# A fused linear-attention and feed-forward kernel: one mask tile, u by a row, refitted fillers, one decay row by DMA, and a new order

## The chip, the cores and the metric

The kernel runs on one core of a Trainium2 chip. The core has five engines that work side by side, each through its own list of instructions in order: PE (TensorE, matrix products and transposes into PSUM), DVE (VectorE, elementwise work and reductions), ACT (ScalarE, exponentials, logarithms and copies), POOL (GpSimd, some elementwise work, and the issue of the loads that convert types) and SP (SyncE, which here issues transfers). Sixteen DMA engines move data for all of them. The metric is device time in microseconds (us). The kernel before takes 171.32 us, the median of three runs (171.07 to 171.39).

## What is computed

There are 4 batches, 8 heads, 768 tokens and 48 dimensions per head. For each batch and head a state of 48x48 is carried along the tokens:

```python
cur = einsum('bhd,bhe->bhde', u * k_t, v_t)
y_t = einsum('bhd,bhde->bhe', r_t, state + cur)
state = w_t[..., None] * state + einsum('bhd,bhe->bhde', k_t, v_t)
```

The result, as 3072 rows of 384, goes through `a = x @ w1`, `b = x @ w2`, `h = (a * b) @ w3`, `out = h @ w_out`, with an inner width of 1024. All tensors come and go in float32.

## The kernel before

**Units.** The 768 tokens are cut into six chunks of 128. A unit is one chunk of one or two batches. There are 13 (`UNITS`): units 0 and 1 are the first chunk of batch 0 and of batch 1 alone; every other unit holds two batches. Tiles have the chunk's 128 tokens on the partitions.

**Attention of a unit t.** Names are those of the steps in the code. `ln_t` (L402) takes the logarithm of the decays w. `cs_t` (L414) sums it along the tokens with a triangular matrix `LT`; in the same step, for units whose state is needed later, eight (or four) matmuls of one column (L419) sum over the whole chunk, and `pc_t` (L426) makes the chunk's decay factors from that, with the channels on the partitions. `ne_t` (L433) is exp of minus the sum and `KRk_t` (L438) multiplies k by it. For r there are two ways. Units in `RAW` form the sum transposed (`csT_t`, L451), its exponential (`et_t`, L457), transpose r itself (`trw_t`) and multiply (`KRw_t`). The others form `iw_t`, `rw_t`, `e_t` and `KRr_t` and then transpose (`trr_t` on PE with the copy `trre_t`, or `dtr_t`, a transposing DMA on SP, from unit 7 on). k goes the same way (`trk_t` and `trke_t`, or `dtk_t` from unit 8 on). `m_t_b` (L549) forms the 128x128 products of all eight heads of one batch, and a strictly triangular mask is laid on them: by one DVE product from PSUM (`msk_t_b`, L568), or by a copy on ACT (`mcp_t_b`) and a second step on POOL or DVE (`maff_t_b`). `rk_t`, `ruk_t`, `dg_t` and `dv_t` give the term with u. `ys_t` adds what the state gives, `yi_t_b` the products with v; `yb_t` puts y together (for the unit in `Y_PE`, PE adds the u term by `yd_t`, and `ybc_t` copies). y is transposed to `xT`, by `yt_t` and `xT_t` or by the transposing DMAs `dty_t_b`. `kv_t`, `T_t`, `S_t` and `Sb_t` carry the state.

**Feed-forward of a unit.** w3 and w_out are first multiplied into one matrix `w34`, block by block: four transposes of w3 in each `wt_f_h`, a copy `w3Te_f`, eight matmuls `wm_f` (L374) and a copy `w34e_f`. Then, per unit, `a_t_g` and `b_t_g` (L688) are products with w1 and w2, `asb_t_g` (ACT) copies a, `abT_t_g` (DVE, L698) multiplies both, `o_t_b` (L704) multiplies by `w34`, `osb_t_b` copies and `st_t_b` (SP) stores.

**The order.** The order of all steps on all engines is written out by hand in the string `ORDER` as `step@engine`; each engine executes its own steps in that order. `BANKS` gives every product its PSUM bank. `warmB@N` stands for N matmuls of zeros (128x512, L302) into bank B; nothing reads them. Loads are steps as well: `win_t`, `kin_t`, `rin_t`, `vin_t` (L329), `w1_h`, `w2_h`, `w3_h` and `wo`, nearly all on POOL's queue, which converts to bfloat16 on the way and issues them in order with POOL's other work. Unit 0's k, r and v are loaded in float32 on SP (`wide_k` and so on, L320) and converted by DVE (`kc_0`, `rc_0`, `vc_0`, L324). u is loaded into all 128 partitions (L294).

Of the kernel before, what the change touches and what calls it, by code (L numbers as in the profile page):

```python
# [37 lines left out]
BANKS = """
cs0=0 ct1=1 cs1=2 tr1=0 ct0=3 tr0=1 ct3=4,5 tk0=2 tk1=6 m0_0=0,1 cs3=2,3 M0_0=0 kv0=7 cs2=5,6 m1_0=0,1 M1_0=1 wt0=4
wt1=5 kv1=6 ct2=0,1 y1=2,3 tk3=0 yt1=2 y0=6,7 tr3=3 tr2=6 tk2=1 m3_1=3,4 m3_0=5,6 M3_0=0 m2_0=0,1 wt2=7 M2_0=1 y3=5,6  # L40
M3_1=2 wt3=0 m2_1=1,2 yt0=3 M2_1=3 wm0=4 wm1=1 wm2=7 wt4=4 wt5=2 y2=5,6 wm3=0 yt3=1 wm4=4 cs4=5,6 wm5=2 cs5=3,4 a0_1=1
yt2=0 kv2=7 a3_2=5 a1_1=6 sa0_1=0 kv3=0 sa1_1=1 tr4=1 a2_2=7 a2_3=6 tk4=0 tr5=3 sa2_3=2 b2_2=2 b2_3=1 b1_1=4 b3_2=6
b0_1=3 sa2_2=1 tk5=4 a1_0=7 a0_0=3 sa1_0=0 a3_0=2 sa0_0=1 a2_1=4 sa3_2=2 b0_0=7 sa2_1=2 m4_0=0,1 m4_1=5,6 M4_0=3
a3_3=3 M4_1=1 wt6=4 b1_0=7 sa3_0=1 y4=0,1 m5_0=5,6 M5_0=2 b2_1=2 sa3_3=0 wt7=7 a3_1=3 b3_0=5 cs6=0,1 b3_1=6 a2_0=7
wm7=2 sa3_1=2 ct6=4,5 sa2_0=1 yt4=3 cs7=0,1 kv4=6 kv5=7 a4_3=3 wm6=4 sa4_3=2 y5=0,1 m5_1=5,6 b4_0=7 M5_1=1 tr6=3
b4_3=2 tk6=5 b2_0=6 a4_0=4 cs8=2,3 sa4_0=2 b3_3=0 a4_2=1 a4_1=4 o0_0=5 sa4_2=2 sa4_1=0 m6_0=6,7 y6=2,3 m6_1=0,1 o2_0=4
M6_1=1 M6_0=2 cs9=0,1 yt5=6 o3_0=7 so0_0=0 so2_0=1 b5_1=6 b4_1=5 a5_1=4 a5_2=0 sa5_1=1 yt6=2 b4_2=1 tk7=3 kv6=4 kv7=5
o3_1=6 so3_0=2 a5_0=2 cs10=3,4 sa5_0=1 a6_3=7 sa5_2=0 b6_3=2 sa6_3=2 b5_0=1 a6_2=0 b5_2=5 a6_1=7 a5_3=1 sa6_1=2 b6_1=3
sa6_2=1 sa5_3=0 o1_0=4 so3_1=0 m7_0=0,1 so1_0=1 m7_1=5,6 y7=2,3 M7_0=1 kv8=7 M7_1=2 o4_0=4 b6_0=0 so4_0=3 cs11=5,6
b5_3=1 b6_2=4 a6_0=2 yt7=3 o5_0=1 a7_2=3 sa6_0=0 so5_0=0 a7_1=4 a7_0=7 sa7_2=1 b7_0=2 sa7_0=2 o2_1=1 a7_3=5 so2_1=1  # L50
sa7_1=2 m9_0=2,3 m8_0=6,7 sa7_3=0 m8_1=0,1 M9_0=2 o5_1=4 M8_1=1 M8_0=3 b7_2=5 so5_1=2 y8=2,3 y9=0,1 m9_1=6,7 M9_1=0
b7_3=4 o4_1=5 cs12=6,7 o6_0=4 so4_1=1 b7_1=2 o6_1=3 o7_1=2 so6_0=3 a8_3=0 so6_1=0 so7_1=2 a8_2=1 a8_0=5 sa8_3=2 b8_3=4
sa8_0=0 b8_2=3 sa8_2=1 b8_0=2 kv10=6 kv9=7 a8_1=0 a9_0=4 sa8_1=2 o7_0=5 b8_1=1 so7_0=1 sa9_0=1 a9_2=3 m10_0=6,7
sa9_2=0 m10_1=4,5 y10=0,1 M10_0=0 a9_1=2 b9_1=3 M10_1=2 sa9_1=2 b9_2=6 o8_1=7 m11_0=4,5 m11_1=2,3 y11=0,1 M11_0=2
o8_0=6 M11_1=0 b9_3=4 a9_3=5 sa9_3=0 a10_3=2 b10_3=3 sa10_3=2 a10_0=5 b10_2=0 sa10_0=0 b10_0=1 so8_1=0 b10_1=2 b9_0=4
so8_0=2 a10_1=3 a10_2=5 a11_3=4 sa10_2=1 a11_2=6 sa10_1=0 b11_2=1 sa11_2=2 o9_1=7 y12=5,6 so9_1=3 m12_1=0,1 m12_0=2,3
sa11_3=1 M12_1=0 o10_1=7 M12_0=2 a11_0=4 so10_1=2 a11_1=0 sa11_0=0 sa11_1=2 b11_1=1 b11_3=7 o9_0=2 b11_0=3 o10_0=4
so9_0=0 o11_1=3 so10_0=1 b12_3=4 so11_1=3 a12_2=2 a12_0=7 sa12_2=0 b12_2=1 sa12_0=1 a12_3=5 b12_0=6 sa12_3=2 a12_1=0
b12_1=3 sa12_1=0 o11_0=2 o12_1=3 so11_0=2 o12_0=4 so12_1=3 so12_0=2
"""  # L60
ORDER = """
table@ACT zeros@DVE u@SP win_0@POOL kin_0@SP rin_0@SP win_1@POOL vin_0@SP rin_1@POOL win_3@POOL kc_0@DVE padlw@DVE
padet@DVE ones@DVE kin_1@POOL mask1@DVE LT@POOL win_2@POOL ln_0@ACT rc_0@DVE rk_0@DVE warm0@18 cs_0@PE padr@DVE
kin_2@POOL padkr@DVE ln_1@ACT uc@ACT warm1@6 csT_1@PE w3_0@POOL pc_0@ACT cs_1@PE ruk_0@DVE et_1@ACT ne_0@ACT
vin_1@POOL pc_1@ACT I128@POOL mask@POOL warm3@9 trw_1@PE csT_0@PE trw_0@PE ln_3@ACT kin_3@POOL ne_1@ACT warm4@3
csT_3@PE KRk_1@DVE KRk_0@DVE rin_3@POOL rk_1@DVE warm6@2 trk_0@PE vc_0@DVE trk_1@PE KRw_1@DVE trke_0@ACT dg_0@DVE
rin_2@POOL et_0@ACT et_3@ACT KRw_0@DVE ruk_1@DVE w3_1@POOL warm7@8 m_0_0@PE trke_1@DVE ln_2@ACT cs_3@PE msk_0_0@DVE
wo@POOL kv_0@PE cs_2@PE vin_3@POOL m_1_0@PE pc_2@ACT ne_2@ACT msk_1_0@DVE warm4@2 wt_0_0@PE w3_2@POOL pc_3@ACT
wt_1_0@PE ne_3@ACT wt_0_1@PE dg_1@DVE vin_2@POOL kv_1@PE csT_2@PE S_0@DVE dv_0@DVE yi_1_0@PE et_2@ACT dv_1@DVE
win_4@POOL S_1@DVE warm7@3 yd_1@PE KRk_3@DVE ybc_1@ACT KRk_2@DVE warm7@2 trk_3@PE w3Te_0@ACT win_5@POOL Sb_0@DVE  # L70
yt_1@PE yi_0_0@PE wt_1_1@PE Sb_1@ACT yb_0@DVE trw_3@PE w3Te_1@ACT trke_3@DVE w1_1@POOL warm1@1 trw_2@PE KRw_3@DVE
trk_2@PE KRw_2@DVE warm4@1 m_3_1@PE rk_3@DVE warm7@1 m_3_0@PE trke_2@DVE mcp_3_0@ACT rin_4@POOL ruk_3@DVE warm7@4
m_2_0@PE wt_2_0@PE maff_3_0@DVE mcp_2_0@ACT ys_3@PE wt_2_1@PE msk_3_1@DVE xT_1@ACT maff_2_0@POOL warm0@1 wt_3_0@PE
warm1@1 wt_3_1@PE dg_3@DVE m_2_1@PE yt_0@PE mcp_2_1@ACT rk_2@DVE kin_4@POOL warm4@3 wm_0@PE ruk_2@DVE maff_2_1@POOL
yi_3_0@PE w3Te_2@DVE wm_1@PE w34e_0@DVE dv_3@POOL dg_2@DVE yi_3_1@PE w3Te_3@ACT wm_2@PE rin_5@POOL yb_3@DVE w34e_1@ACT
wt_4_0@PE xT_0@DVE wt_5_0@PE w2_1@POOL wt_4_1@PE w3Te_4@DVE warm0@1 yi_2_0@PE wm_3@PE kin_5@POOL w34e_2@DVE dv_2@DVE
wt_5_1@PE yi_2_1@PE ln_4@ACT w1_0@POOL w34e_3@DVE yt_3@PE wm_4@PE yb_2@DVE w3Te_5@ACT xT_3@DVE iw_4@ACT cs_4@PE
w2_0@POOL w34e_4@DVE wm_5@PE pc_4@ACT ln_5@ACT ne_4@ACT cs_5@PE w3_3@POOL a_0_1@PE e_4@ACT yt_2@PE pc_5@ACT iw_5@ACT
rw_4@DVE kv_2@PE vin_4@POOL a_3_2@PE ne_5@ACT xT_2@DVE KRr_4@DVE a_1_1@PE asb_0_1@ACT S_2@DVE win_6@POOL kv_3@PE
asb_1_1@ACT KRk_4@DVE trr_4@PE T_3@DVE e_5@ACT a_2_2@PE rw_5@DVE win_7@POOL trre_4@ACT a_2_3@PE KRr_5@DVE trk_4@PE  # L80
S_3@DVE w34e_5@ACT trr_5@PE asb_2_3@ACT rk_4@DVE vin_5@POOL b_2_2@PE Sb_3@ACT ruk_4@DVE trre_5@DVE b_2_3@PE b_1_1@PE
KRk_5@DVE rin_7@POOL b_3_2@PE abT_1_1@DVE b_0_1@PE dg_4@DVE asb_2_2@ACT trk_5@PE kin_6@POOL abT_0_1@DVE a_1_0@PE
trke_5@ACT abT_2_2@DVE a_0_0@PE abT_2_3@DVE asb_1_0@ACT a_3_0@PE rin_6@POOL asb_0_0@ACT trke_4@DVE a_2_1@PE
asb_3_2@ACT b_0_0@PE abT_3_2@DVE asb_2_1@ACT m_4_0@PE abT_0_0@DVE m_4_1@PE mcp_4_0@ACT a_3_3@PE msk_4_1@DVE wt_6_0@PE
Sb_2@ACT b_1_0@PE asb_3_0@ACT maff_4_0@DVE wt_6_1@PE ys_4@PE abT_1_0@DVE dv_4@POOL m_5_0@PE yi_4_0@PE msk_5_0@DVE
# [678 lines left out]
```

## Time and profile before

| | |
|---|---|
| median of three runs | 171.32 us |
| the profiled execution | 171.16 us |
| its span, first to last instruction | 169.4 us |
| PE, PE's weight loads, DVE, ACT, POOL: busy | 162.6, 122.0, 134.1, 89.5, 86.2 us |
| matmuls of zeros | 66, busy 19.9 us |
| moved by DMA | 25.63 MB, mean 151 GB/s |

A profile page has these parts: busy time of each engine; the span in 40 slices of 4.2 us with the busy share of each engine in tenths; the DMA queues; the chain of work that ended last, followed back from the end; the costliest groups of instructions, with mean duration and the idle time ahead of them. Matmuls are pipelined: the mean duration of a matmul in a group contains its latency, and the time that it costs PE is the distance from one start to the next (0.2155 us for 512 columns, 0.1625 for 384, 0.109 for 256, 0.056 for 128, and about 0.025 for very narrow ones, as rows of the chain have it: eight of 512 columns in 1.73 us, eight of 384 in 1.30, 24 of 256 in 2.62, eight of 128 in 0.45). Such a distance is called a slot below. The span leaves out 1.76 us of the profiled execution's time.

### The profile page before, as it was taken

Reading aid. Unit: us, or ns where it says so; the run is one execution under the profiler, and the core shown is the slowest. Engines: PE = TensorE matmul, PEld = TensorE weight load, DVE = VectorE, ACT = ScalarE, POOL = GpSimd, SP = SyncE. Lnnn points to the kernel's source line nnn. Section 1 sums busy time; section 2 is a strip of 40 time slices with the busy share of each in tenths; the row PEclk is TensorE's granted clock in tenths of the full one; section 3 lists DMA queues with packets and bytes.
Section 4 is the critical chain, followed back from the end, with each engine's and each line's share of the span. In section 5 each row is a group of like instructions: output and inputs, shape, how many; then the busy total and the mean of one; then the engine's idle time right before and its main releaser. Section 6 shows DMA issues by size and latency. Waiting matters only on the chain.

```text
span 169.4 us, 4733 instructions
## 1 busy us (share of the span) xinstructions
PE 162.6 (96%) x1998; PEld 122.0 (72%) x1998; DVE 134.1 (79%) x221; ACT 89.5 (53%) x151; POOL 86.2 (51%) x83
## 2 busy tenths in 40 slices
PE   7999999999999999999999999999999799999991
...
DMA  3999999999999999999959999959949944603313
GB/s 80 212 205 182 146 198 189 206 215 153 183 203 217 175 173 167 172 149 174 194 106 90 174 203 236 164 49 109 135 109 141 157 87 109 165 4 95 137 58 130
DMA packets 98837, 25.63 MB, mean 151 GB/s; under 512 B 90880, under 2 KB 96640, under 8 KB 98816
## 3 DMA queue, kind: packets, MB, share of 16 engines
...
## 4 chain that ended last, share of the span: by engine, by line
PE 73%; DVE 11%; DMA 7%; ACT 4%; issue 2%; POOL 1%; SPq 0%; DVEq 0%; ACTq 0%
PE banks L688 28%; PE banks L704 13%; PE banks L302 10%; PE banks L374 6%; DMA vin<-in_v_dram 5%; PE banks L549 3%; DVE abT L698 3%; PE banks L594 2%; PE banks L414 2%; PE banks L510 2%; PE banks L365 1%; DMA out_dram<-osb 1%; DVE dg L528 1%; ACT a_sb L693 1%; PE banks L647 1%
## 5 line engine op out<-in xcount | busy, mean ns | idle before, releaser
L688 PE MATMUL banks<-xT,w_bf 128*128 128x256 bf16 (+1 forms) x624 | 69.7, 264 | 0.5 <-DMA xT<-yb 0.4
L688 PEld LDWEIGHTS <-w_bf 128*128 128x128 bf16 x624 | 55.2, 98 | 7.8 <-issue 1.0
L693 ACT COPY a_sb<-banks 128x512 f32<-128x512 f32 x48 | 27.4, 594 | 27.8 <-PE banks L688 22.5
L698 DVE TENSOR_TENSOR abT<-a_sb,banks 128x512 bf16<-128x512 f32 x48 | 31.6, 681 | 10.4 <-PE banks L688 6.9
L704 PE MATMUL banks<-w,abT 128*128 128x384 bf16 x192 | 34.5, 326 | 0.1
L704 PEld LDWEIGHTS <-abT 128*128 128x128 bf16 x192 | 18.1, 98 | 10.7
L568 DVE TENSOR_TENSOR Mbf<-banks,mask 128x1024 bf16<-128x1024 f32 x17 | 20.4, 1219 | 1.6 <-PE banks L549 1.3
L302 PE MATMUL banks<-zeros 128*128 128x512 bf16 x66 | 19.9, 431 | 1.4 <-DVE zeros L243 1.3
L537 POOL TENSOR_TENSOR dv<-vin,dg 128x768 bf16<-128x768 bf16 x9 | 13.3, 1482 | 15.5 <-DMA vin<-in_v_dram 8.7
L709 ACT COPY osb<-banks 128x384 f32<-128x384 f32 x13 | 6.3, 482 | 21.7 <-PE banks L704 9.2
L329 POOL DMA_DIRECT2D win<-in_w_dram x13 | 15.0, 1157 | 1.1 <-POOLq L748 0.8
L329 POOL DMA_DIRECT2D rin<-in_r_dram x12 | 13.8, 1152 | 2.8 <-DMA w_bf<-in_moe_w_dram 2.5
L402 ACT ACTIVATE lw<-win 128x768 bf16<-128x768 f32 (+1 forms) x13 | 10.5, 811 | 8.7 <-DMA win<-in_w_dram 8.7
L329 POOL DMA_DIRECT2D vin<-in_v_dram x12 | 13.9, 1160 | 2.3 <-DMA w_bf<-in_moe_w_dram 0.9
L329 POOL DMA_DIRECT2D kin<-in_k_dram x12 | 13.8, 1153 | 1.7 <-issue 0.7
L612 DVE TENSOR_TENSOR yb<-banks,dv 128x768 bf16<-128x768 f32 (+1 forms) x12 | 11.1, 921 | 4.4 <-issue 1.8
L302 PEld LDWEIGHTS <-zeros 128*128 128x128 bf16 x66 | 6.5, 108 | 8.2 <-issue 3.8
L433 ACT ACTIVATE NEt<-banks 128x768 bf16<-128x768 f32 (+1 forms) x13 | 9.9, 765 | 3.6 <-PE banks L414 3.6
L663 POOL TENSOR_TENSOR Sst<-Tst,pc 128x384 f32<-128x384 f32 x4 | 3.7, 934 | 15.7 <-DVE Tst L655 15.6
L374 PE MATMUL banks<-wo_bf,w3T 128*128 128x384 bf16 x64 | 11.7, 325 | 0.0
L528 DVE TENSOR_REDUCE dg<-ruk 128x16 f32<-128x768 bf16 (+1 forms) x13 | 11.5, 881 | 0.0
L594 PEld LDWEIGHTS <-Mbf 128*128 128x128 bf16 x192 | 7.8, 96 | 2.5 <-issue 1.1
...
## 6 DMA issues: line engine op xcount, KB each, us to landing
out_dram<-osb SPq DMA_DIRECT2D x24, 192.0 KB, 2.1
...
kin<-in_k_dram POOLq DMA_DIRECT2D x11, 192.0 KB, 7.8
rin<-in_r_dram POOLq DMA_DIRECT2D x11, 192.0 KB, 8.4
vin<-in_v_dram POOLq DMA_DIRECT2D x11, 192.0 KB, 8.7
...
wo_bf<-in_moe_w_out_dram POOLq DMA_DIRECT2D x1, 768.0 KB, 13.5
```

The costliest lines, as they stand in the source:

```text
L302: nc.tensor.matmul(banks[:, at, :], lhsT=zeros[:, :C], rhs=zeros, start=True, stop=True)
L329: QUEUE[eng].dma_start(dst, src)
L374: nc.tensor.matmul(one(f"wm{fi}")[:, :DM], lhsT=w3T[fi % 2][:, gi, :], rhs=wo_bf[:, gi, :], start=(gi == 0), stop=(gi == FI - 1))
L528: nc.vector.reduce_sum(dgs, ruks, axis=AX.X)
L537: e.tensor_mul(dvs, vv, dgs[:, :, None].to_broadcast([C, bh, D]))
L568: nc.vector.tensor_mul(Mbf[bank[f"M{t}_{b}"]], mview(), mask.rearrange("s (j q) t -> s j q t", j=2))
L594: nc.tensor.matmul(o[:, h % 2, b, h // 2, :], lhsT=M[:, h % 2, h // 2, :], rhs=vv[:, b * H + h, :], start=(not c and b == 0 and h < 2), st ...
L612: nc.vector.tensor_add(ybs.rearrange("t b (q e d) -> t e (b q) d", e=2, d=D), yview().rearrange("t e (x d) -> t e x d", d=D), dvs.rearrang ...
L688: nc.tensor.matmul(o[:, f, :], lhsT=wt[:, di, fi * P:(fi + 1) * P], rhs=x[:, di, :T], start=(di == 0), stop=(di == DI - 1))
L693: copier(eng)(a_sb[bank[f"sa{t}_{g}"]], one(f"a{t}_{g}"))
L698: nc.vector.tensor_mul(ab[:, g * per:(g + 1) * per, :T], sa.rearrange("p (f t) -> p f t", t=T), one(f"b{t}_{g}").rearrange("p (f t) -> p f ...
L704: nc.tensor.matmul(one(f"o{t}_{b}")[:, :DM], lhsT=ab[:, fi, b * C:(b + 1) * C], rhs=w34[:, fi, :], start=(fi == 0), stop=(fi == FI - 1))
```

## The change

It has these parts:

- The mask is one 128x128 tile, made by DVE as `LT` minus the identity, and is read eight times in place of a tile of 128x1024 made by a memset and a POOL selection.
- u comes as one row of 384 values, is converted (`uc`), spread over the partitions by a matmul with a row of ones (`ub`) and copied (`ue`).
- Unit 0's float32 tiles and u lie in the space of two `abT` tiles that are used only later; `win_0` and `vin_0` and u are issued by SP, `win_1`, `rin_0` and `kin_0` by ACT, and the conversions of unit 0 are on ACT.
- Units 0 and 2 leave `RAW`; `Y_PE` is unit 0 in place of unit 1; six mask steps in place of seven go by way of a copy on ACT; there are four `a_sb` tiles in place of three.
- The one-column matmuls are a step of their own, `cc_t`. For unit 10 they are left out: `px_10` takes the exponential of the last 32 rows of the sum, and `pd_10` moves the last row to the partitions by DMA.
- The fillers are counted in units of 128 columns: `warmB@N` issues N/4 matmuls of 512 columns and one for the rest. Their number falls from 66 of 512 columns to 144 units of 128.
- `BANKS` and `ORDER` are new throughout. Some code is more general (`BLOCKS`, `DEPTH`) with the same result here.

```diff
-N_ASB = 3
+N_ASB = 4
-RAW = {0, 1, 2, 3, 6}
+RAW = {1, 3, 6}
+ROW_PC = {10}
-POOL_MASK = {(2, 0), (2, 1), (3, 0), (4, 0), (6, 1), (7, 1), (8, 1)}
-Y_PE = {1}
+POOL_MASK = {(3, 0), (5, 0), (6, 1), (7, 1), (9, 1), (11, 1)}
+Y_PE = {0}
...
-    mask = sb.tile([C, 2 * HP, C], BF, name="mask")
+    mask = sb.tile([C, C], BF, name="mask")
-    u_f = sb.tile([C, DM], F32, name="u_f")
-    wide = {(x, t): sb.tile([C, H, D], F32, name=f"wide_{x}{t}") for t in sorted(F32_IN) for x in "krv"}
+    late = [abT[2][i].rearrange("p f t -> p (f t)") for i in (N_AB[2] - 2, N_AB[2] - 1)]
+    u_r = late[0][0:1, 4 * DM:5 * DM]
+    late = [x.bitcast(F32) for x in late]
+    u_f = late[0][0:1, DM:2 * DM]
...
     @op("mask")
     def _(eng):
-        nc.gpsimd.affine_select(mask, mask, compare_op=Alu.is_gt, fill=0.0, base=0, channel_multiplier=-1,
-                                pattern=[[0, 2 * HP], [1, C]])
+        nc.vector.tensor_sub(mask, LT, I128)
...
-        nc.sync.dma_start(u_f, u.rearrange("h d -> (h d)").partition_broadcast(C))
+        QUEUE[eng].dma_start(u_f, u.rearrange("h d -> (h d)").rearrange("(p x) -> p x", p=1))
...
+    @op("ub")
+    def _(eng):
+        nc.tensor.matmul(one("ub")[:, :DM], lhsT=LT[0:1, :], rhs=u_r, start=True, stop=True)
+    @op("ue")
+    def _(eng):
+        copier(eng)(u_bc, one("ub")[:, :DM])
...
     def warm(at, n):
-        for _ in range(n):
-            nc.tensor.matmul(banks[:, at, :], lhsT=zeros[:, :C], rhs=zeros, start=True, stop=True)
+        while n > 0:
+            k = min(n, 4) * C
+            nc.tensor.matmul(banks[:, at, :k], lhsT=zeros[:, :C], rhs=zeros[:, :k], start=True, stop=True)
+            n -= 4
...
+            @op(f"px_{t}")
+            def _(eng):
+                dst = own(prow)[96:].rearrange("t (e d b q) -> t b q e d", e=2, b=nb, q=HP)
+                for b in range(nb):
+                    nc.scalar.activation(dst[:, b, :, :, :D], cs_view()[96:, b].rearrange("t (q e d) -> t q e d", e=2, d=D),
+                                         Act.Exp)
+            @op(f"pd_{t}")
+            def _(eng):
+                QUEUE[eng].dma_start(PC, own(prow)[C - 1:C])
...
-                    nc.vector.tensor_mul(Mbf[bank[f"M{t}_{b}"]], mview(), mask.rearrange("s (j q) t -> s j q t", j=2))
+                    nc.vector.tensor_mul(Mbf[bank[f"M{t}_{b}"]], mview(),
+                                         mask[:, None, None, :].to_broadcast([C, 2, HP, C]))
```

The opening of the old order, up to the first `wm`:

```
table@ACT zeros@DVE u@SP win_0@POOL kin_0@SP rin_0@SP win_1@POOL vin_0@SP rin_1@POOL win_3@POOL kc_0@DVE padlw@DVE
padet@DVE ones@DVE kin_1@POOL mask1@DVE LT@POOL win_2@POOL ln_0@ACT rc_0@DVE rk_0@DVE warm0@18 cs_0@PE padr@DVE
kin_2@POOL padkr@DVE ln_1@ACT uc@ACT warm1@6 csT_1@PE w3_0@POOL pc_0@ACT cs_1@PE ruk_0@DVE et_1@ACT ne_0@ACT
vin_1@POOL pc_1@ACT I128@POOL mask@POOL warm3@9 trw_1@PE csT_0@PE trw_0@PE ln_3@ACT kin_3@POOL ne_1@ACT warm4@3
...
rin_2@POOL et_0@ACT et_3@ACT KRw_0@DVE ruk_1@DVE w3_1@POOL warm7@8 m_0_0@PE trke_1@DVE ln_2@ACT cs_3@PE msk_0_0@DVE
wo@POOL kv_0@PE cs_2@PE vin_3@POOL m_1_0@PE pc_2@ACT ne_2@ACT msk_1_0@DVE warm4@2 wt_0_0@PE w3_2@POOL pc_3@ACT
...
warm1@1 wt_3_1@PE dg_3@DVE m_2_1@PE yt_0@PE mcp_2_1@ACT rk_2@DVE kin_4@POOL warm4@3 wm_0@PE ruk_2@DVE maff_2_1@POOL
```

The opening of the new order, up to the first `wm`, in full:

```
zeros@DVE win_1@ACT win_0@SP padlw@DVE ones@DVE rin_0@ACT u@SP LT@POOL kin_0@ACT vin_0@SP padr@POOL table@ACT
kin_1@POOL rin_1@POOL ln_1@ACT uc@DVE ln_0@ACT padkr@DVE warm0@33 cs_1@PE win_3@POOL ub@PE padpx@DVE cs_0@PE rc_0@ACT
csT_1@PE ue@DVE iw_0@ACT win_2@POOL cc_1@PE cc_0@PE ne_1@ACT ne_0@ACT e_0@ACT I128@POOL KRk_1@DVE kin_2@POOL kc_0@ACT
padet@DVE warm4@19 trk_1@PE et_1@ACT KRk_0@DVE trw_1@PE rw_0@DVE vc_0@ACT rin_3@POOL KRr_0@DVE pc_0@ACT trke_1@ACT
warm5@8 kv_0@PE rk_1@DVE trk_0@PE KRw_1@DVE rk_0@DVE warm6@3 m_1_0@PE vin_1@POOL ln_3@ACT ruk_0@DVE trr_0@PE S_0@DVE
trre_0@DVE trke_0@ACT rin_2@POOL warm7@6 cs_3@PE mask@DVE dg_0@DVE m_0_0@PE dv_0@DVE cc_3@PE ln_2@ACT kin_3@POOL
msk_1_0@DVE ne_3@ACT w3_0@POOL msk_0_0@DVE iw_2@ACT warm7@24 cs_2@PE w3_1@POOL ne_2@ACT ruk_1@DVE warm7@12 yi_0_0@PE
wo@POOL KRk_2@DVE yd_0@PE cc_2@PE ybc_0@ACT kv_1@PE vin_2@POOL e_2@ACT trk_2@PE yt_0@PE pc_3@ACT pc_2@ACT trke_2@ACT
csT_3@PE rw_2@DVE vin_3@POOL et_3@ACT win_4@POOL KRk_3@DVE Sb_0@ACT KRr_2@DVE warm1@27 trk_3@PE dg_1@DVE w3_2@POOL
trr_2@PE trke_3@ACT dv_1@DVE trw_3@PE win_5@POOL rk_3@DVE trre_2@ACT warm2@4 yi_1_0@PE wt_0_0@PE yb_1@DVE rin_4@POOL
wt_0_1@PE pc_1@ACT KRw_3@DVE wt_1_0@PE wt_1_1@PE S_1@DVE m_3_1@PE rk_2@DVE w3Te_1@ACT Sb_1@DVE msk_3_1@DVE w1_1@POOL
warm2@8 wt_3_0@PE w3Te_0@ACT wt_3_1@PE m_2_0@PE m_3_0@PE m_2_1@PE mcp_3_0@ACT msk_2_1@DVE xT_0@ACT yt_1@PE wt_2_0@PE
ruk_2@DVE ys_3@PE xT_1@DVE wt_2_1@PE dg_2@DVE kin_4@POOL wm_1@PE msk_2_0@DVE maff_3_0@POOL wm_0@PE w3Te_3@ACT dv_2@DVE
```

291 lines of the change are left out of this document (148 added, 143 removed).

## The prediction

> **What bounds the kernel now.** I read the page's busy times first, then the slices, then the chain that ended last, and then the timeline around the last of the filler matmuls.
>
> ```profile
> PE 162.6 (96%) x1998; PEld 122.0 (72%) x1998; DVE 134.1 (79%) x221; ACT 89.5 (53%) x151; POOL 86.2 (51%) x83
> PE   7999999999999999999999999999999799999991
> DMA  3999999999999999999959999959949944603313
> L302 PE MATMUL banks<-zeros 128*128 128x512 bf16 x66 | 19.9, 431 | 1.4 <-DVE zeros L243 1.3
> ```
>
> PE is never idle after the first slice, but 66 of its matmuls multiply zeros. They hold the places where it would wait. So PE's share does not say what bounds the first 31 us; the DMA row, full from the second slice on, suggests it. The chain in order of time (start us, us, what):
>
> ```profile
> 1.26 6.93 PE banks L302 x18
> ...
> 14.91 1.73 PE banks L302 x8
> ...
> 30.48 0.65 PE banks L302 x3
> 31.13 1.30 PE banks L374 x8
> ```
>
> The first 18 zeros take 0.385 us each, the eight at 14.91 us 0.216: PE starts at half pace (the granted clock reads 1.00 in every window all the same, so pace must be read from spacing). The last row is `wm_0`, the first matmul group that needs `wo`. After it only one zero matmul is left. The transfers around it, from the list of DMA issues (KB each, us to landing) and the timeline (start, us; the wait in brackets):
>
> ```profile
> u_f<-in_u_dram SPq DMA_DIRECT2D x1, 192.0 KB, 3.8
> wo_bf<-in_moe_w_out_dram POOLq DMA_DIRECT2D x1, 768.0 KB, 13.5
> 16.72 0.94 POOL L348 DMA_DIRECT2D wo_bf<-in_moe_w_out_dram  x1
> 30.48 1.16 POOL L329 DMA_DIRECT2D kin<-in_k_dram  x1 [0.53 <-DMA wo_bf<-in_moe_w_out_dram]
> ```
>
> `wo` is issued at 16.72 and lands 13.5 us later, at 30.2; POOL's next `kin` issue, which waits for that landing, confirms it. PE starts `wm_0` 0.9 us after. So the opening is bound by the queue of loads, and the zeros cover it. From there PE's own work runs nearly without a gap to 165.71 us, with DVE close behind (busy 49.2 of the 50 us from 60 to 110). PE's named waits:
>
> ```profile
> PE banks L594 <- DMA vin<-in_v_dram: 0.9, 1, 0.9
> PE banks L688 <- DMA xT<-yb: 0.4, 1, 0.4
> PE banks L688 <- DVE abT L698: 0.2, 1, 0.2
> ```
>
> Hence my sum: (start of the first `wm`) + (PE work after it) + (stalls after it) + (tail after the last matmul).
>
> **The change, part by part.** The sum is made against the profiled execution, 171.16 us (span 169.4 and 1.76 around it), 0.16 under the median.
>
> *Fillers.* Before: 66 × 0.2155 us = 14.2. After: fills of 144 units of 128 columns, or 36 matmuls' worth, 7.8 us. The 6.5 us less are not a gain by themselves: ahead of the first `wm` they only uncover waiting. Behind it, one zero matmul (0.22 us) goes: −0.22.
>
> *PE's real work.* Units 0 and 2 leave the raw path: 12 matmuls of `csT` go, 12 × 0.056 = 0.67 us. The eight one-column matmuls of `cc_10` go, 8 × 0.025 = 0.20. The row of `u` adds one of 384 columns, 0.16. Sum −0.71. In front of the first `wm` the order puts 10.20 us of real slots where it was 10.71, so behind it there is 0.20 less: −0.20.
>
> *Start of the first `wm`* (now `wm_1`). It needs `wo`. Ahead of `wo` the two kernels load the same tensors, in another order and partly by ACT and SP in place of POOL: all of units 0 and 1, `win`, `kin`, `rin` of 2 and 3, two quarters of w3. Only u changes, from 192 KB spread over 128 partitions to one row of 1.5 KB. Price of those 192 KB: above, the 1.05 us between u's landing and the next one on its queue (4.63 and 5.68); below, nothing, if they only filled the ramp of the first slice (3 tenths busy). I take 0.75, nearer the upper end, since 192 KB at the second slice's 212 GB/s is 0.9. So `wo` lands at 30.19 − 0.75 = 29.45, and `wm_1` starts 0.1 later, at 29.55 where it was 31.13: −1.58. That POOL issues its first load after two memsets (an estimate: 3.0 us where it was 1.35) costs nothing as long as the transfers of ACT and SP keep the engines full until POOL's land, 6.2 us after issue by the `win` of units 0 and 1; these six (u apart five of 192 KB at about 0.95 each, from the landings between 5.68 and 9.63) reach to about 8.5, POOL's first lands at about 9.2. If that gap is lost whole, 0.7 of the 1.58 is gone.
>
> *Is PE there by 29.55?* The last load its chain needs is `kin_3`. Before, everything up to `rin_2` had landed at 23.51; the same set without the first w3 quarter (2.12, from 15.77 to 17.89) and without u's 0.75 gives 20.6. Behind it DVE has, at the mean durations of their groups, KRk_3 0.61, KRr_2 0.70, dg_1 0.54, dv_1 0.55, rk_3 0.55, yb_1 0.56, KRw_3 0.69: 24.8. PE then has m_3_1, eight filler units and the steps up to `wt_2_1`: 0.29 + 0.43 + 2.24 = 2.96, so 27.8. It waits 1.7 us for `wo`. This is the cover for everything moved onto ACT and DVE in the opening (the three casts of unit 0 go to ACT at some 0.5 each; `ue`, rw and KRr of units 0 and 2 come to DVE, 0.55 + 0.71 + 1.35): they cost nothing until the chain slips by more than 1.7 us. On ACT, `ne_1` now queues behind `rc_0`, which waits for `rin_0`; everything on PE after `cc_0` waits for that. The slip is inside the 1.7 if `rin_0` lands by about 8.6, where it landed before.
>
> *DVE and ACT behind the opening.* By the rows DVE sheds the mask memset 0.91, casts 2.87, seven output copies 3.9, and gets one more PSUM mask (1.22); over all, DVE loses about 7.8 us of row time and ACT gains 9.5 on 89.5. The mask as one 128x128 tile read eight times costs nothing by the nearest row: ruk, which reads u over both batches, takes 557 ns against 549 for rk, which does not; above, if the repeat cost what it costs there per row, 18 × 0.01. Between 60 and 110 us, where DVE was full, its load falls only by about 1 in 54, so nothing is counted.
>
> *Row of unit 10.* ACT does two exponentials on 32 partitions (about 0.5 each) and SP one small transfer; the order places it 35 us of PE work ahead of `S_10`, so it is hidden.
>
> *Stalls behind the first `wm`.* Before: 165.71 − 31.13 = 134.58 of which slots take 132.1 (`a` and `b` 528 × 0.109 + 96 × 0.056 = 62.9, `o` 192 × 0.1625 = 31.2, `wm` 64 × 0.1625 = 10.4, all other steps in the order behind it 27.4, one zero 0.2), so 2.45. The 0.9 for `vin` goes: its issue stood 6.7 us of PE work ahead of its first use, now 18.5. What is late next are transfers with less slack, since PE arrives 1.6 us sooner at loads that land 0.75 sooner: `vin_3` (an estimate: 31.44, plus one more `vin` of 1.25 ahead of it, less 0.75: 31.9) feeds `yi_3_0` at 32.4; the third w3 quarter, now behind two `vin` and `win_4`, lands at 29.45 + 2 × 1.25 + 1.8 + 2.5 = 36.2, and PE wants it at 36.9. On SP, `dty_12_0` stands 3.3 us of PE work ahead of `a_12_0` and takes 2.6. Also POOL's mask step `maff_3_0` stands behind a `kin` issue that waits for `wo`, as before: ready at 32.2. All fit, by 0.2 to 0.7 us. I keep 2.45; ends: 1.2 (the two DMA waits go, none come) and 5 (as much again).
>
> *Tail* after the last matmul: unchanged, ACT copy and store.
>
> Sum: −1.58 − 0.20 − 0.22 + 0 = −2.0: 171.16 − 2.0 = **169.2 us**.
>
> **The rivals.**
> A. *Loads land no earlier* (the gap before POOL's first landing, or u's bytes were free). `wm_1` starts at 30.3; −0.83 − 0.42: 169.9. For it: the ramp slice is only 3 tenths busy.
> B. *PE falls back to half pace.* Before, PE was never idle for 1 us in the opening; now 6.5 us of filler are gone, with 1.7 us idle right before `wm_1`. If the pace drops, one slow stretch costs what the first one did: 6.93 − 18 × 0.2155 = 3.05 us, 172.2 us, slower. It decides once a stretch of about 2.1 us is lost at or after `wm_1`. For it: the new fills are sparse. Against: no row shows how long an idle stretch it takes. The Trainium skill, TensorE: Matmul & The Clock Gate, "Why this matters for your kernels", says that gaps up to about 3 us are safe, and its Part 4 that transposes do not count as activity; from 20.6 us to `wm_1` PE does mostly transposes, so by the first rule the sum stands, by the second B happens. No run shown can decide.
> C. *The new order stalls in the full stretch of DVE* (60 to 110 us): stalls at 5.0 in place of 2.45, 171.7. For it: DVE has nothing to spare there; against: its load is a little smaller.
> D. *Fewer stalls*: only 1.2, 167.9.
>
> **How the numbers follow.** Forecast (168.3 to 169.8) 0.42, A 0.13, D 0.10, C 0.20, B 0.15. About 0.2% (0.34 us) is what a measurement of this kernel can tell. Faster: forecast, A, D and a little of C, 0.67. Same: part of C, 0.07. Slower: B and the rest of C, 0.26. The range runs from D's lower edge, 167.6, to B with a small surplus, 172.4.
>
> **What would show it.** `wo` landing at 29.2 to 29.7 with `wm_1`'s first matmul right behind it and 1 to 2 us of PE idle ahead: the opening is right. `wo` at 30 or later: A. `w34` groups of eight taking 2.6 us in place of 1.30, or 0.107 us between 128-column matmuls after 20 us: B. PE waits for DVE's abT or a mask that sum to more than 3 us: C. The prediction is wrong from the root if PE reaches `wm_1` after `wo` has landed; then DVE's or ACT's chain bounds the opening, and each microsecond beyond 29.5 is one of the result.

## The result, and the profile after

The changed kernel takes **176.36 us** (median of 4 runs, 175.65 to 176.45); the kernel before took 171.28 beside it. The ratio is 1.029, with a 95% interval of 1.026 to 1.032: slower by 5.1 us, where 169.2 us was forecast. The profiled execution took 176.31 us, its span 174.6.

From the changed kernel's page: the busy times, and the slices of PE and of its clock.

```profile
PE 158.5 (91%) x1948; PEld 119.0 (68%) x1951; DVE 131.2 (75%) x210; ACT 97.2 (56%) x165; POOL 86.0 (49%) x83
PE   7699879999999999989993999799899989999991
PEclk9999999999999999999999699999999999999999
```

PE is busy for less time than before (158.5 against 162.6 us) in a longer span. Two things stand out: a slice at 3 tenths and the clock's 6 beside it, both between 91 and 100 us. The opening is not the place of the loss. Its timeline (start, us; the wait in brackets):

```profile
27.75 2.77 PE L400 MATMUL banks<-wo_bf,w3T 128*128 128x384 bf16 x16
28.00 1.19 POOL L355 DMA_DIRECT2D kin<-in_k_dram  x1 [2.92 <-DMA wo_bf<-in_moe_w_out_dram]
```

`wo` lands at 27.71 (issued 13.73, 13.98 later) and the first `wm` starts at 27.75; the timeline before has it at 30.97 (the chain, which leaves out what overlaps, at 31.13). To see where that gain went I compared the two traces at equal amounts of real matmul work left (start-to-start slots, zeros at nothing). After minus before, in us and good to some tenths, since the order of the work differs: −3.4 at the first `wm`, −2.9 at 50, −2.0 at 76, −0.6 at 90.5, +1.2 at 94.8, **+3.9 at 100.4**, **+5.2 at 110.8**, +6.3 at 128, +5.3 at the end. So the opening gained more than forecast; 2.8 of it went in small waits up to 90 us; and about 6 us were lost between 90 and 111.

That stretch, in the timeline of the changed kernel:

```profile
84.07 1.57 ACT L460 ACTIVATE prow<-banks 32x384 f32<-32x384 f32 x2
...
85.67 0.48 ACT L751 COPY osb<-banks 128x384 f32<-128x384 f32 x1
...
86.17 0.36 SPq L756 DMA_DIRECT2D out_dram<-osb  x1
86.36 1.22 POOL L355 DMA_DIRECT2D win<-in_w_dram  x1
...
86.65 3.29 SPq L532 DMA_TRANSPOSE KRT<-KR  x2
...
94.44 0.62 PE L592 MATMUL banks<-KRT 64*128 64x128 bf16 x16 [2.26 <-DMA KRT<-KR]
...
94.49 0.56 DVE L527 TENSOR_TENSOR KR<-rw,Et 128x768 bf16<-128x768 bf16 x1 [3.08 <-DMA KRT<-KR]
```

The first line is `px_10`, the two exponentials of the row of unit 10. Behind them on ACT stands `osb_1_0`; behind that, on SP, its store and the DMA transposes `dtr_7` and `dtr_8`. At 86.36, just ahead of `dtr_7`, POOL issues the load `win_12`. The chain in order of time has the price (start, us, what):

```profile
85.60 1.05 PE banks L746 x7
86.65 7.75 DMA KRT<-KR
...
94.49 0.42 DVE KR L527
```

`dtr_7` takes 7.75 us to land; before, its two transposes took 4.2 and 4.7. PE waits 2.26 us for it at `m_7`. Worse, DVE waits 3.08: `KRr_9` writes the `KR` buffer that `dtr_7` still reads (there are two). The order of work around this place, which the prediction had looked at only for `px_10`'s own cover:

```
asb_5_0@ACT Sb_5@ACT ys_6@PE dg_7@DVE osb_0_0@ACT dv_6@POOL o_1_0@PE ne_10@ACT px_10@ACT maff_6_1@DVE yi_6_0@PE
a_5_1@PE abT_5_3@DVE yi_6_1@PE osb_1_0@ACT o_3_0@PE ruk_8@DVE asb_5_1@ACT st_1_0@SP yb_6@DVE dtr_7@SP b_5_1@PE
Sb_6@DVE rw_9@DVE yt_6@PE dtr_8@SP osb_3_0@DVE b_4_2@PE dv_7@POOL xT_6@DVE o_2_0@PE abT_5_1@DVE st_3_0@SP st_3_1@SP
win_12@POOL dg_8@DVE st_0_0@SP b_5_0@PE pd_10@SP osb_2_0@ACT abT_4_2@DVE dtk_8@SP iw_10@ACT a_6_3@PE KRr_9@DVE
```

### The profile page after: what moved, and what is told of

It reads as the page before. It is cut to its first block, busy times and chain, and to the rows that moved or that the text cites. A ratio compares the mean times of both kernels' runs of the same rounds, so it can differ in the third digit from the quotient of the medians.

```text
span 174.6 us, 4648 instructions
## 1 busy us (share of the span) xinstructions
PE 158.5 (91%) x1948; PEld 119.0 (68%) x1951; DVE 131.2 (75%) x210; ACT 97.2 (56%) x165; POOL 86.0 (49%) x83
## 4 chain that ended last, share of the span: by engine, by line
PE 52%; DMA 17%; DVE 11%; POOL 8%; ACT 5%; issue 3%; SPq 1%; ACTq 0%; DVEq 0%
PE banks L730 26%; PE banks L746 13%; DMA vin<-in_v_dram 9%; DMA KRT<-KR 4%; DMA out_dram<-osb 4%; DVE abT L740 4%; PE banks L400 4%; PE banks L638 2%; POOL rin L355 2%; ACT a_sb L735 2%; POOL kin L355 1%; SPq L666 1%; POOL win L355 1%; DVE Mbf L611 1%; ACT NEt L476 1%
## 5 line engine op out<-in xcount | busy, mean ns | idle before, releaser
L730 PE MATMUL banks<-xT,w_bf 128*128 128x256 bf16 (+1 forms) x624 | 70.8, 265 | 3.0 <-DVE Mbf L611 1.2
L746 PE MATMUL banks<-w,abT 128*128 128x384 bf16 x192 | 35.7, 334 | 0.0
L746 PEld LDWEIGHTS <-abT 128*128 128x128 bf16 x192 | 18.6, 100 | 11.2 <-issue 1.0
L751 ACT COPY osb<-banks 128x384 f32<-128x384 f32 x20 | 9.5, 480 | 27.6 <-PE banks L746 19.3
L611 DVE TENSOR_TENSOR Mbf<-banks,mask 128x1024 bf16<-128x1024 f32 x18 | 21.7, 1218 | 2.8 <-PE banks L592 2.8
L580 POOL TENSOR_TENSOR dv<-vin,dg 128x768 bf16<-128x768 bf16 x10 | 15.8, 1585 | 12.0 <-DVE dg L571 7.7
L355 POOL DMA_DIRECT2D win<-in_w_dram x11 | 13.0, 1186 | 0.6 <-issue 0.5
L327 PE MATMUL banks<-zeros 128*128 128x512 bf16 (+3 forms) x35 | 10.5, 419 | 1.5 <-DVE zeros L258 1.3
L592 PE MATMUL banks<-KRT 64*128 64x128 bf16 x192 | 8.2, 218 | 2.5 <-DMA KRT<-KR 2.3
L606 POOL TENSOR_SCALAR_AFFINE_SELECT Mbf<-Mbf 128x1024 bf16<-128x1024 bf16 x4 | 4.5, 1131 | 10.9 <-ACT Mbf L598 10.9
L481 DVE TENSOR_TENSOR KR<-kin,NEt 128x768 bf16<-128x768 bf16 (+1 forms) x13 | 7.9, 604 | 2.4 <-DMA kin<-in_k_dram 2.1
```

Source lines behind the costliest of these rows:

```text
L327: nc.tensor.matmul(banks[:, at, :k], lhsT=zeros[:, :C], rhs=zeros[:, :k], start=True, stop=True)
L355: QUEUE[eng].dma_start(dst, src)
L580: e.tensor_mul(dvs, vv, dgs[:, :, None].to_broadcast([C, bh, D]))
L611: nc.vector.tensor_mul(Mbf[bank[f"M{t}_{b}"]], mview(), mask[:, None, None, :].to_broadcast([C, 2, HP, C]))
L730: nc.tensor.matmul(o[:, f, :], lhsT=wt[:, di, fi * P:(fi + 1) * P], rhs=x[:, di, :], start=(di == 0), stop=(di == DI - 1))
L746: nc.tensor.matmul(one(f"o{t}_{b}")[:, :DM], lhsT=ab[:, fi, k * C:(k + 1) * C], rhs=w34[:, fi, :], start=(fi == 0), stop=(fi == FI - 1))
```

## The experiments

Theory: the load and the transposes in flight together cost the time. Rivals: the fall of the clock; the row of unit 10 itself; the opening. Each ratio is to runs of the kernel before on the same chip; their medians are 171.1 to 171.4 us, so times from different chips can be compared to about 0.3 us. A time is the median of a run's executions; everything from a trace is of one of them.

**1. The load out of the way.**

```diff
-win_12@POOL dg_8@DVE st_0_0@SP
+dg_8@DVE st_0_0@SP
...
-vin_7@POOL abT_4_1@DVE
+vin_7@POOL win_12@POOL abT_4_1@DVE
```

> The changed kernel with one step moved: POOL issues win_12 right behind vin_7 (about 76.6 us) in place of behind dv_7 (86.36 us, 0.3 us ahead of SP's dtr_7). Theory T: PE's wait of 2.3 us for KRT, DVE's wait of 3.1 us for the KR buffer, and the lower granted clock behind them (0.64 and 0.51 in 96 to 100 us) all come from dtr_7 and dtr_8 landing 7.75 and 6.99 us after issue, because win_12's load moves at the same time. Then dtr_7 lands within 5 us of its issue, PE's wait for KRT is under 0.5 us, the granted clock stays at 1.00, and the time is 171.5 us (170.5 to 172.7). Rival R: the order on DVE is too slow there whatever the transposes do; the wait turns into one for DVE and the time stays above 174.5 us.

170.22 us (169.81 to 170.31), ratio 0.994 (0.991 to 0.996). Timeline:

```profile
86.57 2.71 SPq L532 DMA_TRANSPOSE KRT<-KR  x2
...
92.03 0.62 PE L592 MATMUL banks<-KRT 64*128 64x128 bf16 x16
```

The row of unit 10 is still there and SP issues the transposes at the same time, but they land in 3.1 to 3.3 us and nothing waits at `m_7`. The time is 0.3 us below the expected band. One moved load turns 5 us slower into 1 us faster.

**2. Zeros in the wait**, so that PE does not rest (44 units of 128 columns ahead of `m_7_0`).

```diff
-rk_9@DVE m_7_0@PE
+rk_9@DVE warm5@44 m_7_0@PE
```

> The changed kernel with 11 matmuls of zeros (512 columns, 2.4 us) put right ahead of m_7_0, where PE stands idle for 2.3 us. They can't shorten the wait. If the fall of the granted clock behind it follows from PE's idling, the clock stays at 1.00, the matmuls from 96 to 100 us run at full pace and the time falls by 1.2 to 2.0 us, to 174.3 to 175.1. If the clock has nothing to do with it, 176.3 within 0.4.

174.85 us (174.79 to 175.08), ratio 1.022 (1.019 to 1.024): inside the expected band, 1.5 us below the changed kernel, with the clock at 1.00 throughout. That seemed to price the clock's fall at 1.5 us; the traces say otherwise. At equal work left, this run is 1.5 us ahead of the changed kernel at first (98.94 against 100.44), but level with it three microseconds on (102.26 against 102.38) and up to 119 (118.83 against 118.92), because here PE then waits for DVE (PE's waits from 90 to 112 us: in us total, times, longest):

```profile
PE banks L730 <- DVE Tst L700: 1.2, 1, 1.2
PE banks L730 <- DVE Mbf L611: 1.2, 1, 1.2
```

In the changed kernel the first of these waits is missing: PE is late enough by itself. So the fall was hidden behind DVE. The 1.5 us at the end came later: the changed kernel's PE loses 0.75 us at 123.5, waiting for a transposing DMA of y, and 0.96 at 142.3, waiting for an output copy on ACT that itself waits 2.89 us for a store; this one does neither. Why not is left open.

**3. u's bytes back**: a second load of u, spread over 128 partitions as before, that nobody reads.

```diff
+    u_pad = sb.tile([C, DM], F32, name="u_pad")
+    @op("upad")
+    def _(eng):
+        QUEUE[eng].dma_start(u_pad, u.rearrange("h d -> (h d)").partition_broadcast(C))
```

> The changed kernel with one load more: u into all 128 partitions, 192 KB, on SP behind the row of u; nothing reads it. It prices the part of the change that narrows u. By the prediction's term wo lands 0.75 us later (27.7 becomes 28.4) and wm_1 starts as much later; the end is 0 to 0.75 us later, 176.3 to 177.1. By rival A the bytes are free, wo lands at 27.7 within 0.2 and the time is 176.3.

`wo` lands at 28.83 instead of 27.71, 1.12 us later. In the eleven traces that load as the changed kernel does, `wo` lands anywhere from 27.55 to 28.44 (mean 27.85), so the 192 KB are worth about 1 us, and no nearer than 0.4 to 1.3: not free, and my 0.75 is inside. The time, 175.87 us (175.74 to 177.26), is not above the changed kernel's, and below both expected bands: a microsecond gained in the opening is gone by the wait at `m_7`, where `dtr_7` lands at 95.06 here.

**4. The row of unit 10 undone**: the column form of the prefix for unit 10, as before; no `px_10`, no `pd_10`.

```diff
-ROW_PC = {10}
+ROW_PC = set()
...
-cs_10@PE abT_4_3@DVE
+cs_10@PE cc_10@PE abT_4_3@DVE
-ne_10@ACT px_10@ACT maff_6_1@DVE
+ne_10@ACT pc_10@ACT maff_6_1@DVE
-b_5_0@PE pd_10@SP osb_2_0@ACT
+b_5_0@PE osb_2_0@ACT
```

> The changed kernel with unit 10's decay factors made as before (cc_10 right behind cs_10, pc_10 in the place of px_10, no pd_10 and no padding of prow). pd_10 stands on SP between the transposes and the stores of the slow stretch. If it and the two exponentials on 32 partitions cost nothing, as predicted, 176.3 within 0.4 us; if they hold up SP or ACT there, 0.5 to 1.5 us faster.

169.73 us (169.22 to 171.32, 9 runs, four of them 170.7 or more), ratio 0.994 (0.990 to 0.997): far below either expectation. Timeline:

```profile
84.64 0.48 ACT L751 COPY osb<-banks 128x384 f32<-128x384 f32 x1 [0.45 <-PE banks L746]
...
85.14 0.36 SPq L756 DMA_DIRECT2D out_dram<-osb  x1
...
85.62 2.76 SPq L532 DMA_TRANSPOSE KRT<-KR  x2
...
86.22 1.22 POOL L355 DMA_DIRECT2D win<-in_w_dram  x1
```

Without the exponentials `osb_1_0` comes a microsecond sooner, and SP's transposes are issued 0.6 us ahead of the load instead of 0.3 behind it: `dtr_7` lands in 3.23 us. So the row that I had priced at nothing is worth 6.6 us here. Whether by its delay or by itself, the next three runs tell.

**5. Only the order**: the row stays, `px_10` goes behind `osb_1_0`.

```diff
-ne_10@ACT px_10@ACT maff_6_1@DVE
+ne_10@ACT maff_6_1@DVE
...
-osb_1_0@ACT o_3_0@PE
+osb_1_0@ACT px_10@ACT o_3_0@PE
```

> The changed kernel with one move: unit 10's two exponentials (px_10, 1.57 us on ACT) are issued behind osb_1_0 instead of ahead of it, so osb_1_0, its store on SP and the transposes dtr_7 and dtr_8 queued behind that store come about 1.5 us sooner, ahead of win_12's load. The row of unit 10 stays, with its DMA pd_10. Theory (order decides: what costs the time is that dtr_7 is issued behind the load): dtr_7 issued near 85.1, landing 3.1 to 3.5 us later, no wait at m_7, and the time 169.6 to 171.2 us. Rival (the row itself costs it: its exponentials and its DMA, wherever px_10 stands): 175 to 176.5 us.

169.74 us (169.41 to 170.43), ratio 0.991 (0.988 to 0.993).

```profile
84.58 0.48 ACT L751 COPY osb<-banks 128x384 f32<-128x384 f32 x1 [0.52 <-PE banks L746]
...
85.08 1.57 ACT L460 ACTIVATE prow<-banks 32x384 f32<-32x384 f32 x2
85.08 0.36 SPq L756 DMA_DIRECT2D out_dram<-osb  x1
...
85.56 2.74 SPq L532 DMA_TRANSPOSE KRT<-KR  x2
...
86.35 1.22 POOL L355 DMA_DIRECT2D win<-in_w_dram  x1
```

The same exponentials and the same DMA, one step further down ACT's queue, cost nothing that can be measured.

**6. Only the delay**: run 4 with two exponentials of the same shape in `px_10`'s old place, into a tile that nobody reads.

```diff
-ne_10@ACT pc_10@ACT
+ne_10@ACT pad_10@ACT pc_10@ACT
```

> The kernel with the row of unit 10 undone (169.73 us; no exponentials of a row, no pd_10), plus two exponentials of the same 32x384 shape in px_10's old place that write to a tile nobody reads: only the delay on ACT ahead of osb_1_0 is put back. Theory (the delay alone does it: it puts dtr_7 a fraction of a microsecond behind win_12's issue, and then transposes and load run together and land late): dtr_7 issued near 86.7, landing 6.5 us or more later, a wait of 1.5 us or more at m_7, and 174 to 176.8 us. Rival (the row's own DMA, or its tile, has to be there too): 169.5 to 171 us.

173.22 us (172.87 to 174.55), ratio 1.013 (1.008 to 1.018): 3.5 us over run 4, so the delay alone brings the wait back, but only half of the 6.6 us. In the profiled execution some 0.6 us of that has another source: `wo` lands at 28.34 in it, and the first `wm` starts 0.6 us later than in run 4's. Load and transposes are issued at the same moment here (86.92 and 86.91), and `dtr_7` takes 6.07 us:

```profile
86.91 3.15 SPq L541 DMA_TRANSPOSE KRT<-KR  x2
86.92 1.22 POOL L355 DMA_DIRECT2D win<-in_w_dram  x1
...
93.07 0.56 DVE L536 TENSOR_TENSOR KR<-rw,Et 128x768 bf16<-128x768 bf16 x1 [1.10 <-DMA KRT<-KR]
```

**7. Is the other half `pd_10`?** The changed kernel with `pd_10` issued behind `dtr_9`.

```diff
-b_5_0@PE pd_10@SP osb_2_0@ACT
+b_5_0@PE osb_2_0@ACT
...
-dtr_9@SP cs_11@PE
+dtr_9@SP pd_10@SP cs_11@PE
```

> The changed kernel with one move: pd_10, the DMA that spreads the row of unit 10 (issued at 92.05 on SP, landing 97.05), is issued behind dtr_9 instead, when the transposes of units 7 and 8 have landed. The delay alone gave 173.22 us, the changed kernel 176.36. Theory (the delay's exact place makes the difference: the load issued 0.29 us ahead of dtr_7 and not with it, transposes landing 7.75 us after their issue and not 6.07, then the clock's fall): the time stays at 175.5 to 176.6 us. Rival (pd_10's DMA in flight with them costs the rest): 173 to 174.5 us.

176.45 us (176.08 to 178.25), ratio 1.032 (1.026 to 1.039): no. With the load again 0.29 us ahead, `dtr_7` takes 7.86 us and DVE waits 3.2. What is left to tell 173.22 from 176.36 is the offset of load and transposes, 0.01 us against 0.29; no run puts the load 0.3 us ahead without the row, so that half is argued from the landing times and not isolated.

**8. The load further ahead**: run 4 with `win_12` ahead of `dv_7`.

```diff
-dv_6@POOL o_1_0@PE
+dv_6@POOL win_12@POOL o_1_0@PE
...
-win_12@POOL dg_8@DVE
+dg_8@DVE
```

> The kernel with the row of unit 10 undone (169.73 us), and one move the other way: win_12's load stands ahead of dv_7 on POOL, so it is issued near 84.6 instead of 86.22, about a microsecond ahead of dtr_7 (85.6). Theory (a load issued just ahead stretches the transposes): dtr_7 lands 6 to 8 us after its issue instead of 3.23, a wait of 1.5 us or more comes back at m_7, and the time is 173 to 176.5 us. Rival (the row of unit 10 was the cause and the load's place means nothing): 169.4 to 170.3 us, dtr_7 landing in under 4 us.

My expectation fell: 170.02 us (169.90 to 170.16), ratio 0.993. The load is issued at 84.44, 1.29 us ahead of `dtr_7`, which does take longer (5.44 us), but lands at 91.17. DVE comes to `KRr_9` only at 92.10 here, and at 91.19 in run 4, where PE comes to `m_7` at 91.97. So a stretched transpose costs nothing until it passes the moment at which DVE wants the buffer, 91.2 to 92.1. The load moves mostly before the transposes do: the list of DMA packets has 214 KB of it in flight from 87 to 88 us, ahead of nearly all of theirs.

Put together, for `dtr_7` and its load (offset is the load's issue minus `dtr_7`'s):

| kernel | offset, us | `dtr_7` to landing | lands at | DVE waits | time, us |
|---|---|---|---|---|---|
| load out of the way | far ahead, landed | 3.27 | 89.84 | 0 | 170.22 |
| px_10 behind osb_1_0 | +0.79 | 3.20 | 88.75 | 0 | 169.74 |
| row undone | +0.60 | 3.23 | 88.84 | 0 | 169.73 |
| delay only | +0.01 | 6.07 | 92.98 | 1.10 | 173.22 |
| changed | −0.29 | 7.75 | 94.40 | 3.08 | 176.36 |
| zeros in the wait | −0.30 | 7.75 | 94.31 | 3.1 | 174.85 |
| pd_10 late | −0.29 | 7.86 | 94.76 | 3.2 | 176.45 |
| u's bytes back | −0.30 | 8.03 | 95.06 | 3.4 | 175.87 |
| load further ahead | −1.29 | 5.44 | 91.17 | 0 | 170.02 |

In runs 10 to 12 below, `dtr_7` is again issued 0.6 us ahead of the load, and lands in 3.19 to 3.24 us.

**9. All loads earlier.** Run 4 with `win_12` as in run 1, and `vin_11` and `vin_12` moved up, away from the later transposes.

```diff
-vin_10@POOL m_9_1@PE
+vin_10@POOL vin_11@POOL m_9_1@PE
...
-rin_12@POOL S_8@DVE
+rin_12@POOL vin_12@POOL S_8@DVE
```

> The kernel with the row of unit 10 undone, win_12's load right behind vin_7's, and vin_11 and vin_12 right behind vin_10 and rin_12 (issued near 104 to 107 instead of 117.9 and 119.1), so that no load is in flight with the transposes of units 11 and 12 either. Theory (transposes in flight with loads are what still costs around 120 to 137): KRT landings there 3.1 to 4.2 instead of 4.1 to 6.2 us, and 168.9 to 169.6 us. Rival (nothing waits for them there; the waits left are those of DVE and ACT): 169.5 to 170.1 us.

A miss: 172.15 us (171.69 to 172.58), ratio 1.006 (1.003 to 1.008). At equal work left this trace is behind run 4's by 1.0 us at 106, 2.2 at 110, 2.9 at 122 and 3.1 at the end. So most was lost before any transpose was waited for, and to something else: each issue of a load keeps POOL for about 1.2 us, and with two more of them in front POOL's mask step of unit 9 starts at 108.68 where run 4 has it at 106.33. PE waits for that step:

```profile
108.68 1.47 POOL L606 TENSOR_SCALAR_AFFINE_SELECT Mbf<-Mbf 128x1024 bf16<-128x1024 bf16 x1
...
110.20 0.37 PE L638 MATMUL banks<-vin,Mbf 128*128 128x48 bf16 x8 [1.27 <-POOL Mbf L606]
```

The late landings show a second time as well. `vin_12` now stands just ahead of two other transposes; they take 7.3 to 7.6 us, and DVE waits for one of them:

```profile
107.53 1.15 POOL L355 DMA_DIRECT2D vin<-in_v_dram  x1
...
108.81 1.24 SPq L547 DMA_TRANSPOSE KRT<-KR  x1
110.15 2.62 SPq L532 DMA_TRANSPOSE KRT<-KR  x1
...
117.50 0.56 DVE L527 TENSOR_TENSOR KR<-rw,Et 128x768 bf16<-128x768 bf16 x1 [1.02 <-DMA KRT<-KR]
```

**10. The fillers out**: run 4 without any zeros behind the first 33 units.

```diff
-padet@DVE warm4@19 trk_1@PE
+padet@DVE trk_1@PE
...
-warm2@8 wt_3_0@PE
+wt_3_0@PE
```

> The kernel with the row of unit 10 undone, without any zero matmul behind the first 33 (111 quarter-matmuls of 128 columns removed at nine places up to 36 us). Theory (they only stand in waits, which last as long without them, and TensorE's pace does not hang on them): granted clock near 1 through the opening, 169.2 to 170.0 us. Rival (without them PE falls to half pace behind a wait in the opening, as it did at 96 to 100 us in the changed kernel): the granted clock below 0.9 in a stretch of 2 us or more before 40 us, and 170.8 to 173 us.

171.03 us, but spread from 169.37 to 174.71 over 6 runs, far wider than any other kernel; without the two longest (174.62 and 174.71) the ratio is 0.995 (0.991 to 1.000). Its windows (from:to us, length, busy time of PE, PEld, DVE, ACT, POOL, then the granted clock):

```profile
6.00:8.00 2.00, 0.41 (x13) 0.32 (x9) 0.33 (x1) 2.00 (x6) 2.00 (x3) 1.00 2.29 193
8.00:9.00 1.00, 0.41 (x5) 0.41 (x6) 0.82 (x5) 1.00 (x3) 1.00 (x2) 0.79 1.01 212
9.00:10.00 1.00, 1.00 (x16) 0.75 (x15) 0.97 (x4) 0.82 (x3) 1.00 (x2) 0.50 1.05 220
...
16.00:17.00 1.00, 0.97 (x21) 0.92 (x19) 0.37 (x1) 0.58 (x2) 1.00 (x2) 0.50 2.71 144
```

PE's rests of 2.18 us (up to 8.59) and of 1.64 and 0.63 (from 12.8) are each followed by 3.4 us at half clock. The half of the expectation on the clock went to the rival. The price went to neither in the profiled execution (170.39): the first `wm` starts at 28.28, only 0.5 us later than in run 4, although `wo` lands no later (27.55).

**11. The first loads back on their old queues**, on run 4.

```diff
-zeros@DVE win_1@ACT win_0@SP padlw@DVE ones@DVE rin_0@ACT u@SP LT@POOL kin_0@ACT vin_0@SP padr@POOL table@ACT
+zeros@DVE u@SP win_0@POOL kin_0@SP rin_0@SP win_1@POOL vin_0@SP padlw@DVE ones@DVE LT@POOL padr@POOL table@ACT
```

> The kernel with the row of unit 10 undone, and the first loads back on the queues of the kernel before: win_0 and win_1 on POOL, kin_0, rin_0 and vin_0 on SP behind u, none on ACT. It asks where the opening's gain beyond u's bytes is from (wo landed 2.48 us earlier than before, and u's 192 KB measured 1.1). Theory (spreading the first loads over three queues starts the stream earlier): wo lands 0.8 to 1.6 us later than 27.71, and the time is 170.0 to 171.3 us. Rival (only bytes and order count): wo lands within 0.4 us of 27.71, 169.4 to 170.1 us.

173.18 us (172.75 to 174.53), ratio 1.013 (1.008 to 1.018): slower than either theory said. `wo` lands at 28.35, 0.64 us later than in run 4 but inside the 27.55 to 28.44 of the new queues, so this run does not show that the queues move it. The first `wm` waits until 31.87, 3.5 us behind `wo`. What I had missed is in the list of PE's and ACT's waits in the first 40 us:

```profile
ACT lw L431 <- DMA win<-in_w_dram: 5.6, 1, 5.6
...
PE banks L443 <- ACT lw L431: 3.3, 1, 3.3
```

`win_1` lands at 7.67 from POOL where it lands at 4.6 from ACT's queue, and everything on PE starts from it. The pace of PE adds to it: behind this wait PE stays at half pace, up to 13.97 us, where run 4 is at full pace from 5.34. The same five zeros (start, us), here:

```profile
10.09 2.19 PE L327 MATMUL banks<-zeros 128*128 128x512 bf16 x5
```

and in run 4:

```profile
6.35 1.19 PE L327 MATMUL banks<-zeros 128*128 128x512 bf16 x5
```

PE is 3.1 us later than in run 4 at its first real matmul, 4.3 at 13.9 us and 4.1 at the first `wm`. In this run PE's chain bounds the opening, not `wo`. The trace is of the slowest of its four executions, 174.53 us.

**12. Two of the remaining waits.** Run 4 with `cs_12` behind `o_5_0` and `cc_9` behind `kv_6`.

```diff
-cs_12@PE abT_7_2@DVE o_5_0@PE
+abT_7_2@DVE o_5_0@PE cs_12@PE
...
-cc_9@PE b_4_3@PE trke_7@DVE pc_9@ACT asb_5_2@ACT rk_8@DVE kv_6@PE
+b_4_3@PE trke_7@DVE asb_5_2@ACT rk_8@DVE kv_6@PE cc_9@PE pc_9@ACT
```

> The kernel with the row of unit 10 undone, and two moves against the longest PE waits that are left behind 60 us: cs_12 behind o_5_0 (it waits 1.0 us at 111.5 for yb_8 on DVE to free its banks), cc_9 behind kv_6 with pc_9 behind asb_5_2 (0.69 us at 76.3, for ACT). Theory (these waits are on the path and what follows keeps its slack): 168.2 to 169.2 us. Rival (the time is only waited for at the next place, or transposes and loads then meet in a worse way): 169.3 us or more.

169.52 us (169.23 to 170.27), ratio 0.990 (0.986 to 0.993): faster than both kernels, but not told apart from run 4 or 5, so it went to the rival. In its trace the two waits are gone and others stand in their place (0.40 at 78.5, 0.72 at 116.4).

## Why the prediction was wrong

**The step that failed: "Row of unit 10 ... so it is hidden."** Its own result is hidden, as I said. What I did not price is who stands behind `px_10` on ACT: `osb_1_0`, then SP's store, then `dtr_7`. The 1.57 us of exponentials moved `dtr_7` from 0.6 us ahead of a 384 KB load to 0.3 us behind it. Runs 5 and 6 show that this delay is the cause (169.74 with the row and without the delay; 173.22 with the delay and without the row), run 1 that the load is its partner (170.22 with both and the load elsewhere). Why the delay alone gave 3.5 us and delay and row together 6.6 is put down to 0.3 us of offset, which no run varied alone.

**How 3 us of wait become 6.** The delay of DVE's steps, changed kernel against run 4, is 3.3 us behind `KRr_9` at 94.5 us and 6.2 at 108. DVE is full there, so nothing is made up. The rest is in its timeline, in the changed kernel:

```profile
98.10 1.44 DVE L565 TENSOR_TENSOR ruk<-rk,u_bc 128x768 bf16<-128x768 bf16 x1
99.47 1.82 DVE L527 TENSOR_TENSOR KR<-rw,Et 128x768 bf16<-128x768 bf16 x1
...
106.39 1.82 DVE L519 TENSOR_TENSOR rw<-rin,iw 128x768 bf16<-128x768 bf16 x1
```

and the same three steps with the row undone:

```profile
94.80 0.54 DVE L565 TENSOR_TENSOR ruk<-rk,u_bc 128x768 bf16<-128x768 bf16 x1
95.26 0.55 DVE L527 TENSOR_TENSOR KR<-rw,Et 128x768 bf16<-128x768 bf16 x1
...
101.50 0.55 DVE L519 TENSOR_TENSOR rw<-rin,iw 128x768 bf16<-128x768 bf16 x1
```

They cost 0.90 + 1.27 + 1.27 = 3.4 us more; 0.6 is won back where DVE no longer waits for PE, so 3.3 + 3.4 − 0.6 = 6.1. In the changed kernel they run beside POOL's own steps on SBUF:

```profile
98.04 1.10 POOL L606 TENSOR_SCALAR_AFFINE_SELECT Mbf<-Mbf 128x1024 bf16<-128x1024 bf16 x1 [10.46 <-ACT Mbf L598]
99.11 1.76 POOL L580 TENSOR_TENSOR dv<-vin,dg 128x768 bf16<-128x768 bf16 x1
...
106.29 1.49 POOL L580 TENSOR_TENSOR dv<-vin,dg 128x768 bf16<-128x768 bf16 x1
```

With the row undone, POOL's `dv` steps fall beside DVE steps that read one input from PSUM (`abT`, which takes 0.68 us either way, and the mask products), and it is POOL's mask step that is stretched (2.03 us for 1.10). The delay-only run has the same three long steps (1.44, 1.82, 1.82): its DVE is 1.9 us behind run 4's at `KRr_9`, 1.1 of it the wait, and 4.7 at 107 us, of which 3.5 are left in the time. The Trainium skill, SBUF — State Buffer, "Who interferes with whom", states that a DVE instruction with two SBUF inputs contends with a GpSimd instruction that reads SBUF, as an exclusive lock, and that the order of issue decides who blocks. These rows agree: 0.55 against 1.82 us. That it is a lock, no run here isolates.

The other steps:

- *Start of the first `wm`*, 29.55 in the sum, was 27.75: the gain of 1.58 was 3.2. `wo` came 2.48 us sooner, about 1 of it by u's bytes (run 3, priced 0.75); the rest is not accounted for, since run 11 moved `wo` by no more than it scatters. "PE there by 27.8" came out by luck in part: `kin_3` landed at 18.89 in place of 20.6, and PE then waited 0.88 us for ACT's copy of a mask, which the sum did not have. So there was no wait of 1.7 us for `wo`: PE and `wo` arrive together. What keeps PE in time is `win_1`, 3 us sooner on ACT's queue (run 11).
- *Stalls behind the first `wm`*, kept at 2.45, were about 2.45 + 3.4 + 5.3 = 11.2. They grew ahead of the collision too: losses of 0.59 at 30.5 (for `vin_3`, which lands at 31.12), 0.39 at 54.3, 0.41 at 57.8, 0.69 at 76.4 and 0.36 at 87.3, 2.4 us in all, took most of the 2.8 lost up to 90 us. (These are distances between starts beyond a slot; the timeline, whose durations hold a latency, shows some 0.17 less of each.)
- Without the collision the kernel comes near the forecast: the row undone gives 169.73, px_10 behind osb_1_0 169.74, where 169.2 was forecast and 168.3 to 169.8 was the range. That is luck, not a sum that held: the opening gained some 1.6 us more than priced, and the stalls behind it took about as much again.
- *Rival A* fell, since the loads do land earlier, and *rival D* too, since the stalls grew.
- *Rival B* did occur (the granted clock was 0.986 to 0.990 in all four executions), but at 96.6 us and not in the opening, and it was hidden. In the opening PE did mostly transposes from 19.6 us to the first `wm`, and the clock stayed at 1.00. The windows of the changed kernel:

```profile
95.00:96.00 1.00, 0.56 (x35) 0.56 (x28) 1.00 (x3) 0.27 (x1) 0.00 (x0) 1.00 1.07 398
96.00:97.00 1.00, 0.76 (x13) 0.61 (x6) 1.00 (x2) 1.00 (x3) 0.00 (x0) 0.77 1.25 264
97.00:98.00 1.00, 1.00 (x6) 0.59 (x4) 1.00 (x3) 0.96 (x2) 0.00 (x0) 0.50 0.10 22
```

  PE is at half clock for some 3.4 us and covers a wait for DVE with it. In the run with u's bytes back the clock stays at 1.00 behind a wait of 2.6 us, and the time is no better (175.87); of run 7's executions the one without a fall (granted clock 1.000) took 176.08 us, one with it (0.990) 176.21.
- *Rival C* had place and sign right (the stretch where DVE is full), but neither its cause nor its size: 171.7 us for general stalls, against 176.36 by one late transpose.
